# A sparse-attention and mixture-of-experts kernel: third gathers issued behind what frees their buffer, later zeros, and a first expert that reads no earlier results

## The chip, the cores and the metric

The kernel runs on one core of one Trainium2 chip. The metric is device time in microseconds (us) of one execution. TensorE (PE) multiplies matrices, VectorE (DVE) and ScalarE (ACT) do elementwise work, GpSimd (POOL) here issues all indirect DMAs (gathers and scatters by a list of row indices), and SyncE (SP) issues all other DMAs. Every engine works through its own instruction list in order: an instruction that waits holds up everything behind it on that engine.

## What is computed

Attention with two sparse masks over 8 batches of 576 tokens (8 heads of 64), then a mixture of 8 experts with the two best experts per token. Cut to what matters:

```python
scores = where(masks, scale * q @ k.T, -1e9)         # heads 0-3: a band of 32; heads 4-7: every 32nd key
x = softmax(scores) @ v                              # as 4608 tokens x 512
noisy = x @ w_gate + log1p(exp(x @ w_noise)) * noise # 4608 x 8
top2 = argpartition(-noisy, 2, axis=1)[:, :2]        # and their softmax: top2_w
out = zeros(4608, 512)
for e in range(8):
    for k in range(2):
        mask = top2[:, k] == e
        out[mask] += top2_w[mask, k, None] * (relu(x[mask] @ w1[e]) @ w2[e])
```

w1 is 512x1024 and w2 1024x512 for each expert.

## The kernel before

**Attention.** 32 units of work (batch, pair of heads, kind of mask). A unit loads q, k, v, transposes on PE, multiplies, takes exponentials on ACT, multiplies by v, and stores its part of x to DRAM (`x_dram`, L663). After the four units of a batch, `route` computes the gate and writes, by 12 indirect scatters on POOL (L824), the entries (token, weight) of that batch into each expert's list in DRAM (`tab`).

**Experts.** The list of an expert is cut into steps ("jobs"), listed in `SUBS` as (start, whole blocks of 128 tokens, tail, batches that must be known: `hb`). Seven jobs need only the first batches and are run while attention goes on. In order: job 0 (expert 0, 2 blocks, hb 2), job 1 (expert 0, 2 blocks, hb 4), job 2 (expert 1, 2 blocks, hb 4), job 3 (expert 1, 3 blocks, hb 5), jobs 4 to 6 (expert 2, 3, 2 and 2 blocks, hb 7). 25 more jobs need all 8 batches; 14 of these have a third block (two whole blocks and a third or a tail of 64). A job does the following:

- `gather` (L908): loads the list (L918), makes indices, and gathers the rows of x into tiles `xg`, one per block. The ring of `xg` has two places. Early jobs use one gather per block (L973), the others four (L959).
- `transposes` (L981): per block, transposes on PE into a PSUM bank (L998, early jobs) or on DVE (L1002, the others), and splits the result into a high part `xhi` (ACT, L1009) and a low part `xlo` (DVE, L1011). Rings `xhi`, `xlo` have one place, so they wait for the first layer of the job before.
- `layer1` (L1037), then `layer2` per block (L1099) on PE. Weights are loaded (L889, L892) and split in the same way (L894, L895).
- `previous` (L1077): gathers the rows of `out` that are to be added to. `weighted` (DVE, L1124): `out row + weight * product`. `scatter` (L1129): writes the rows back to `out`.
- The output is first filled with zeros, in 12 stores of 384 rows (L1183, 786432 bytes each, on SP). A gather or a scatter of the first `hb * 576` rows of `out` needs the zeros of these rows.

**The order of the work.** It is written down once, when the program is built. Each piece has an engine, a planned duration, a rank and what it depends on; `issue_all` simulates the engines with these durations and emits the pieces in the order in which they start in this plan. Among the pieces of an engine that could start within 120 ns of the first, the lowest rank goes first. Attention ranks are 10 per unit (40 per batch), expert ranks start at `ER` = 1000000. A piece also has a planned time before which it doesn't start (`t0`); a store of zeros has rank `ER - 1` and is `bulk`, which lets it start only where the planned load of the DMA engines has nearly run out. The semaphores are put in afterwards from what the emitted instructions read and write. So where the plan did not know of a dependency, the instruction waits in its place in the engine's list.

Three places matter here. When a tile is taken from a full ring, the plan makes the piece wait for the users that the tile to be replaced has *at that moment*:

```python
if len(r.hist) >= r.k:
    self.deps += r.hist[-r.k].users
```

In `gather`, all blocks of a job take their `xg` in one go, before `transposes` has made the pieces that read the first of them. For early jobs the list and its `gix` have the rank of the expert, while the list's load has the rank `20 * NP * (hb - 1) + 10 * NP` (NP = 2), which lies among attention's. And `previous` is made for every block, with `others` as the scatters of the other experts so far, which is an empty list for jobs 0 and 1.

Of the kernel before, what the change touches and what calls it, by code (L numbers as in the profile page):

```python
# [9 lines left out]
F32 = mybir.dt.float32  # L10
# [5 lines left out]
ALU = mybir.AluOpType  # L16
# [6 lines left out]
def kernel(  # L23
# [12 lines left out]
    nc = tc.nc  # L36
    B, H, S, D = q.shape
# [5 lines left out]
    NP = HL // 2  # L43
# [230 lines left out]
    def dve(n):  # L274
        return 75 + 1.04 * n

    def dma(fn, nbytes, rank, eng="SP", **kw):
        return Piece(eng, 690 if eng == "SP" else GAP, fn, rank, lat=nbytes, **kw)
# [137 lines left out]
    R = {}  # L416
# [461 lines left out]
            R[f"w{layer}{part}"] = ring(wring, [128, 512], F32R, f"w{layer}{part}", NF)  # L878
    R["wraw"] = ring(wring, [128, 512], F32, "wraw", 5)
    ER = 1000000  # L880
    ZC = 384

    def weights_of(e, layer, i, rank, turn=None):
# [18 lines left out]
    def experts(zero):  # L902
# [2 lines left out]
        known_tab = {n: [x for b in range(n) for x in scatters[b]] for n in range(1, B + 1)}  # L905
        G_, XH, HT = {}, {}, {}

        def gather(n, rank):  # L908
            e, (start, nb, tail, hb) = jobs[n]
            known = hb * S  # L910

            whole = hb < B
# [39 lines left out]
            if not whole:  # L952
                Piece("POOL", 360 if tail else 230, xindices, rank, read=[tx] + ([tx2] if tail else []), alloc=[gx],
                      expert=True)
            xs = []
            for i in () if whole else range(nb + (tail > 0)):
                xg = R["xg"].new()
                for g in range(4 if i < nb else tail // 32):
                    dma(lambda o, i=i, g=g, xg=xg: nc.gpsimd.indirect_dma_start(  # L959
                        out=xg.t[:, g, :], out_offset=None, in_=x_dram[:4 * known, :],  # L960
                        in_offset=bass.IndirectOffsetOnAxis(ap=gx.t[:, i, g:g + 1], axis=0)),
                        65536, rank, eng="POOL", read=[gx], after=known_stores[hb], expert=True,
                        **({"write": [xg]} if g else {"alloc": [xg]}))
                xs.append(xg)

            def indices(o):
                nc.gpsimd.tensor_scalar(gi.t[:, :nb], tb.t[:, :nb, 0], known - 1, None, op0=ALU.min)
                if tail:
                    nc.gpsimd.tensor_scalar(gi.t[:tail, nb:nb + 1], tb.t[:tail, nb, 0:1], known - 1, None, op0=ALU.min)
            Piece("POOL", 300 if tail else 170, indices, rank, read=[tb], alloc=[gi], expert=True)  # L970
            for i in range(nb) if whole else ():
                xg = R["xg"].new()
                dma(lambda o, i=i, xg=xg: nc.gpsimd.indirect_dma_start(  # L973
                    out=xg.t.rearrange("p g c -> p (g c)"), out_offset=None,
                    in_=x_dram.rearrange("(t q) c -> t (q c)", q=4)[:known, :],
                    in_offset=bass.IndirectOffsetOnAxis(ap=gi.t[:, i:i + 1], axis=0)),
                    262144, rank, eng="POOL", read=[gi], after=known_stores[hb], expert=True, alloc=[xg])
                xs.append(xg)
            G_[n] = (tb, gi, xs)

        def transposes(n, rank):  # L981


            e, (start, nb, tail, hb) = jobs[n]
            xh, xl = R["xhi"].new(), R["xlo"].new()
            XH[n] = (xh, xl)
            for i in range(nb + (tail > 0)):
                xg = G_[n][2][i]
                rows = 128 if i < nb else tail
                ng = rows // 32  # L990
                cols = slice(128 * i, 128 * i + rows)
                if hb < B:
                    xr = Slot()

                    def tr(o, xg=xg, xr=xr):
                        xv = xg.t.rearrange("p g c -> p (g c)").rearrange("p (x c) -> p c x", c=ND)
                        for c in range(ND):
                            nc.tensor.transpose(xr.t[:, 128 * c:128 * c + 128], xv[:, c, :], ident)  # L998
                    Piece("PE", 108 * ND, tr, rank, read=[xg], psum=xr, expert=True)
                else:  # L1000
                    xr = R["xr"].new()
                    Piece("DVE", 8 * rows, lambda o, xg=xg, xr=xr, ng=ng, rows=rows: nc.vector.transpose(  # L1002
                        xr.t.rearrange("p (c x) -> p c x", c=ND)[:, :, :rows].rearrange("p c (g i) -> p g c i", g=ng),
                        xg.t[:, :ng, :].rearrange("p g (i c) -> p g c i", c=ND)), rank, read=[xg], alloc=[xr], expert=True)
                how = "write" if i else "alloc"

                def view(xr=xr, rows=rows):
                    return xr.t.rearrange("p (c x) -> p c x", c=ND)[:, :, :rows]
                Piece("ACT", act(4 * rows), lambda o, view=view, cols=cols: nc.scalar.copy(  # L1009
                    xh.t[:, :, cols], view()), rank, read=[xr], expert=True, **{how: [xh]})  # L1010
                Piece("DVE", dve(4 * rows), lambda o, view=view, cols=cols: nc.vector.tensor_tensor(  # L1011
                    xl.t[:, :, cols], view(), xh.t[:, :, cols].bitcast(F32), ALU.subtract),
                      rank, read=[xr, xh], expert=True, **{how: [xl]})

        counts = {}

# [55 lines left out]
        def previous(n, i, rank, others):  # L1072
            e, (start, nb, tail, hb) = jobs[n]
            pv, gi = R["prev"].new(), G_[n][1]
            known = hb * S
            rows = 128 if i < nb else tail
            dma(lambda o: nc.gpsimd.indirect_dma_start(  # L1077
                out=pv.t[:rows, :], out_offset=None, in_=out[:known, :],
                in_offset=bass.IndirectOffsetOnAxis(ap=gi.t[:rows, i:i + 1], axis=0)),
                rows * 2048, rank, eng="POOL", read=[gi], alloc=[pv],  # L1080
                after=others + zero[:-(-known // ZC)], expert=True)
            return pv

        def layer2(n, i, rank, pv):
# [2 lines left out]
            rows = 128 if i < nb else tail  # L1087
            cols = slice(128 * i, 128 * i + rows)
            ps, tb = Slot(), G_[n][0]
            half = rows < 128  # L1090
            if half:

# [27 lines left out]
                Piece("PE", len(part) * 216, mm, rank, read=rd, expert=True, **({"write": [ps]} if c else {"psum": ps}))  # L1120

            def weighted(o):
                for r in range(0, 2 * rows if half else rows, rows):
                    nc.vector.scalar_tensor_tensor(pv.t[:rows, :], ps.t[r:r + rows, :], tb.t[:rows, i, 1:2].bitcast(F32),  # L1124
                                                   pv.t[:rows, :], op0=ALU.mult, op1=ALU.add)
            Piece("DVE", (1 + half) * dve(512), weighted, rank, read=[ps, tb, pv], write=[pv], expert=True)

            def scatter(o):
                st = nc.gpsimd.indirect_dma_start(  # L1129
# [4 lines left out]
                out_scatters[e].append(st)  # L1134
                return st
            out_done[e].append(dma(scatter, rows * 2048, rank, eng="POOL", read=[pv, tb], expert=True))

        def turn(n):
            hb = jobs[n][1][3]
            return None if hb == B else 20 * NP * (hb - 1) + 10 * NP  # L1140

        W2 = {}
        gather(0, ER)
# [36 lines left out]

    for c in range(NTOK // ZC):
        zero.append(dma(
            lambda o, c=c: nc.sync.dma_start(out[ZC * c:ZC * c + ZC, :].rearrange("(p c) (a d) -> p (c a) d", p=128, a=4),  # L1183
                                             zeros[:, None, :].to_broadcast([128, 4 * ZC // 128, 128])), 786432,
            ER - 1, t0=26000 + 10000 * c + 35000 * (c >= 5), bulk=True))
    LL = {0: loads(0, 0), 1: loads(1, 10)}
    KQ = {0: prep(0, LL[0], 0)}
    for u in range(NU):
# [93 lines left out]
```

## Time and profile before

| | us |
|---|---|
| runs shown: median (lowest to highest, 3 runs) | 1108.83 (1102.39 to 1113.18) |
| the profiled execution | 1104.51 |
| its span, first to last instruction | 1102.8 |
| PE busy in it | 1064.4 (97%) |
| DVE, ACT, POOL busy | 607.6, 432.8, 553.8 |

The three runs lie 1% apart. The profiled execution is near the lower end of them. A busy time is the time in which at least one instruction of that engine ran; PE's is modelled at the ends of its matmuls, and matmuls overlap. PEld is the loading of weights into PE. The granted clock (PEclk) is 1.00 at 2.4 GHz; a stretch that shows 0.57 was for a part of it at 1.2 GHz.

### The profile page before, as it was taken

The page shows a single profiled execution, that of the slowest core. Times are in us where ns is not written, and L with a number is a line of the kernel's source. Part 1 is how long each engine was busy: PE and PEld are TensorE (multiplying, and loading weights), DVE is VectorE, ACT ScalarE, POOL GpSimd, SP SyncE. Part 2 cuts the span into 40 slices and gives each one's busy share as a digit, 9 for nine tenths or more (in the row PEclk, how much of TensorE's full clock was granted, in tenths as well). Part 3 has the DMA queues.
Part 4 walks back from the last instruction along what each step waited for, and adds up shares of the span by engine and source line. Part 5 has one row for each costly group of instructions (what it writes and reads, how often), then busy time and mean ns, then how long its engine had stood idle before and what let it go on. Part 6 is the DMA issues. An engine that isn't in the chain of part 4 may idle for free.

```text
span 1102.8 us, 23359 instructions
## 1 busy us (share of the span) xinstructions
PE 1064.4 (97%) x8645; PEld 938.3 (85%) x8645; DVE 607.6 (55%) x1606; ACT 432.8 (39%) x1131; POOL 553.8 (50%) x734
## 2 busy tenths in 40 slices
PE   8898899999799999999999999999999999999995
PEld 7677678889688989898998989898988898898994
DVE  7789976776465223655673456345534553474341
ACT  6689975677353212423341224113312331142120
POOL 1045543510763455656676555655656464657530
PEclk8999999999899999999999999999999999999998
DMA  8999998887534332455554236223622452253210
GB/s 173 230 212 230 240 237 228 218 238 199 144 103 138 91 104 77 135 148 149 156 168 141 71 101 189 79 70 106 185 81 64 121 166 76 69 158 97 72 59 23
DMA packets 169482, 152.93 MB, mean 139 GB/s; under 512 B 52651, under 2 KB 137131, under 8 KB 169348
## 3 DMA queue, kind: packets, MB, share of 16 engines
q1 hardware_dynamic: 145028, 92.30, 33.4%
q0 software_dynamic: 24320, 58.87, 17.7%
q8 instruction: 82, 1.34, 0.5%
q14 instruction: 52, 0.43, 0.1%
HBM read 112.76 MB, written 39.39 MB: 138 GB/s over the span
## 4 chain that ended last, share of the span: by engine, by line
PE 82%; DVE 5%; issue 5%; DMA 4%; ACT 3%; POOL 0%; POOLq 0%; DVEq 0%; SPq 0%
PE bankE L1099 5%; PE bankF L1099 5%; PE bankG L1099 5%; PE bankC L1099 5%; PE bankG L1037 5%; PE bankF L1037 5%; PE bankA L1099 5%; PE bankH L1037 5%; PE bankC L1037 5%; PE bankA L1037 5%; PE bankD L1099 4%; PE bankB L1037 4%; PE bankD L1037 4%; PE bankE L1037 4%; PE bankH L1099 4%
## 5 line engine op out<-in xcount | busy, mean ns | idle before, releaser
L959 POOL DMA_INDIRECT xg<-x_dram,gxx x240 | 241.4, 1006 | 105.1 <-issue 55.7
L1129 POOL DMA_INDIRECT out_dram<-prev,tabt x80 | 82.1, 1026 | 103.7 <-DVE prev L1124 45.9
L1077 POOL DMA_INDIRECT prev<-out_dram,gix x80 | 77.3, 966 | 92.1 <-issue 39.5
L824 POOL DMA_INDIRECT tab<-ent,addr x96 | 92.2, 960 | 57.9 <-issue 15.6
L1002 DVE STREAM_TRANSPOSE xr<-xg 128x512 f32<-128x512 f32 (+1 forms) x64 | 66.3, 1037 | 12.7 <-DMA xg<-x_dram,gxx 11.2
L1009 ACT CAST xhi<-xr 128x512 fp32r<-128x512 f32 (+1 forms) x64 | 37.8, 591 | 69.9 <-DVE xr L1002 69.9
L894 ACT CAST w2hi<-wraw 128x512 fp32r<-128x512 f32 x80 | 47.4, 619 | 29.2 <-PE bankA L1108 7.4
L895 DVE TENSOR_TENSOR w1lo<-wraw,w1hi 128x512 fp32r<-128x512 f32 x80 | 54.7, 686 | 3.5 <-ACT w1hi L894 1.0
L895 DVE TENSOR_TENSOR w2lo<-wraw,w2hi 128x512 fp32r<-128x512 f32 x80 | 52.7, 684 | 3.5 <-ACT w2hi L894 2.2
L1011 DVE TENSOR_TENSOR xlo<-xr,xhi 128x512 fp32r<-128x512 f32 (+1 forms) x64 | 42.1, 658 | 18.4 <-ACT xhi L1009 17.2
L894 ACT CAST w1hi<-wraw 128x512 fp32r<-128x512 f32 x80 | 49.0, 614 | 1.4 <-DMA wraw<-in_moe_w_dram 1.2
L973 POOL DMA_INDIRECT xg<-x_dram,gix x16 | 16.8, 1050 | 58.4 <-PE bankD L998 42.8
L1056 ACT ACTIVATE hhi<-bankG 128x256 fp32r<-128x256 f32 (+2 forms) x34 | 14.3, 421 | 70.9 <-PE bankG L1037 70.9
L1037 PE MATMUL bankG<-xhi,w1hi 128*128 128x256 f32 (+3 forms) x136 | 41.2, 303 | 0.0
L1037 PE MATMUL bankG<-xhi,w1lo 128*128 128x256 f32 (+3 forms) x136 | 40.3, 296 | 0.0
L1037 PE MATMUL bankG<-xlo,w1hi 128*128 128x256 f32 (+3 forms) x136 | 40.1, 295 | 0.0
L1037 PE MATMUL bankF<-xhi,w1hi 128*128 128x256 f32 (+3 forms) x132 | 39.9, 302 | 0.0
L1037 PE MATMUL bankH<-xhi,w1hi 128*128 128x256 f32 (+3 forms) x132 | 39.7, 301 | 0.0
L1037 PE MATMUL bankA<-xhi,w1hi 128*128 128x256 f32 (+3 forms) x132 | 39.6, 300 | 0.0
L1037 PE MATMUL bankC<-xhi,w1hi 128*128 128x256 f32 (+3 forms) x132 | 39.6, 300 | 0.0
L1037 PE MATMUL bankF<-xhi,w1lo 128*128 128x256 f32 (+3 forms) x132 | 39.4, 298 | 0.0
L1037 PE MATMUL bankF<-xlo,w1hi 128*128 128x256 f32 (+3 forms) x132 | 39.3, 298 | 0.0
(666 smaller groups left out, 3573.1 us busy)
## 6 DMA issues: line engine op xcount, KB each, us to landing
wraw<-in_moe_w_dram SPq DMA_DIRECT2D x160, 256.0 KB
out_dram<-zeros SPq DMA_DIRECT2D x12, 768.0 KB
ks<-in_k_dram SPq DMA_DIRECT2D x15, 320.0 KB
qs<-in_q_dram SPq DMA_DIRECT2D x15, 320.0 KB
vraw<-in_v_dram SPq DMA_DIRECT2D x30, 160.0 KB
raw<-in_k_dram SPq DMA_DIRECT2D x16, 288.0 KB
v_l<-in_v_dram SPq DMA_DIRECT2D x16, 288.0 KB
raw<-in_q_dram SPq DMA_DIRECT2D x16, 288.0 KB
```

What stands on the lines that cost most here:

```text
L824: st = nc.gpsimd.indirect_dma_start(out=tab, out_offset=bass.IndirectOffsetOnAxis(ap=s["addr"].t[:, t, kk:kk + 1], axis=0), in_=s["ent"].t ...
L894: Piece("ACT", act(512) + 30, lambda o: nc.scalar.copy(hi.t, raw.t), rank, read=[raw], alloc=[hi], expert=True)
L895: Piece("DVE", dve(512), lambda o: nc.vector.tensor_tensor(lo.t, raw.t, hi.t.bitcast(F32), ALU.subtract), rank, read=[raw, hi], alloc=[lo] ...
L959: dma(lambda o, i=i, g=g, xg=xg: nc.gpsimd.indirect_dma_start(out=xg.t[:, g, :], out_offset=None, in_=x_dram[:4 * known, :], in_offset=bas ...
L973: dma(lambda o, i=i, xg=xg: nc.gpsimd.indirect_dma_start(out=xg.t.rearrange("p g c -> p (g c)"), out_offset=None, in_=x_dram.rearrange("(t ...
L1002: Piece("DVE", 8 * rows, lambda o, xg=xg, xr=xr, ng=ng, rows=rows: nc.vector.transpose(xr.t.rearrange("p (c x) -> p c x", c=ND)[:, :, :row ...
L1009: Piece("ACT", act(4 * rows), lambda o, view=view, cols=cols: nc.scalar.copy(xh.t[:, :, cols], view()), rank, read=[xr], expert=True, **{h ...
L1011: Piece("DVE", dve(4 * rows), lambda o, view=view, cols=cols: nc.vector.tensor_tensor(xl.t[:, :, cols], view(), xh.t[:, :, cols].bitcast(F ...
L1037: nc.tensor.matmul(ps.t[:, :width], a.t[:, 128 * d:128 * d + 128], c.t[:, d, :width], start=(m == 0), stop=(m == len(todo) - 1))
L1077: dma(lambda o: nc.gpsimd.indirect_dma_start(out=pv.t[:rows, :], out_offset=None, in_=out[:known, :], in_offset=bass.IndirectOffsetOnAxis( ...
L1099: nc.tensor.matmul(ps.t, HT[n, f][p[0]].t[:, cols], W2[n][f][p[1]].t, start=(m == 0), stop=(m == len(todo) - 1))
L1129: st = nc.gpsimd.indirect_dma_start(out=out[:known, :], out_offset=bass.IndirectOffsetOnAxis(ap=tb.t[:rows, i, 0:1], axis=0), in_=pv.t[:ro ...
```

## The change

Four edits.

1. `gather` now makes only the first two blocks of a job. The third is made by a function `rows_of`, which `transposes` calls after it has made the pieces of the block whose place the third takes. Nothing else about the gather changes.
2. In early jobs, the index computation and the gathers get the rank that the load of their list has (`turn(n)`), instead of the expert's.
3. The 12 stores of zeros get new earliest times in the plan. Before: 26, 36, 46, 56, 66, 111, 121, 131, 141, 151, 161, 171. After: 95, 105, 115, 140, 150, 160, 185, 195, 215, 228, 240, 280 (in thousands of ns).
4. Jobs 0 and 1 no longer gather rows of `out`: `previous` returns an empty tile, and `weighted` writes weight times product into it. In the plan this piece now waits for the zeros.

```diff
+    ZERO_AT = (95, 105, 115, 140, 150, 160, 185, 195, 215, 228, 240, 280)
...
         def gather(n, rank):
             e, (start, nb, tail, hb) = jobs[n]
+            rank = rank if hb == B else turn(n)
...
-            xs = []
-            for i in () if whole else range(nb + (tail > 0)):
+            def rows_of(i):
                 xg = R["xg"].new()
+                if whole:
+                    dma(lambda o: nc.gpsimd.indirect_dma_start(
...
+                        262144, rank, eng="POOL", read=[gi], after=known_stores[hb], expert=True, alloc=[xg])
+                    return xg
                 for g in range(4 if i < nb else tail // 32):
...
-                xs.append(xg)
+                return xg
+            xs = [] if whole else [rows_of(i) for i in range(2)]
...
-            for i in range(nb) if whole else ():
-                xg = R["xg"].new()
...
-            G_[n] = (tb, gi, xs)
+            if whole:
+                xs = [rows_of(i) for i in range(2)]
+            G_[n] = (tb, gi, xs, rows_of)
...
                       rank, read=[xr, xh], expert=True, **{how: [xl]})
+                if i + 2 < nb + (tail > 0):
+
+                    xs.append(rows_of(i + 2))
...
             pv, gi = R["prev"].new(), G_[n][1]
+            if not others:
+                return pv
...
+            first = jobs[n][0] == jobs[0][0] and hb < B
...
             def weighted(o):
-                for r in range(0, 2 * rows if half else rows, rows):
+                if first:
+                    nc.vector.tensor_scalar(pv.t, ps.t, tb.t[:, i, 1:2].bitcast(F32), None, op0=ALU.mult)
+                for r in () if first else range(0, 2 * rows if half else rows, rows):
...
-            Piece("DVE", (1 + half) * dve(512), weighted, rank, read=[ps, tb, pv], write=[pv], expert=True)
+            Piece("DVE", (1 + half) * dve(512), weighted, rank, expert=True,
+                  **({"read": [ps, tb], "alloc": [pv], "after": zero[:-(-known // ZC)]} if first else
+                     {"read": [ps, tb, pv], "write": [pv]}))
...
-            ER - 1, t0=26000 + 10000 * c + 35000 * (c >= 5), bulk=True))
+            ER - 1, t0=ZERO_AT[c] * 1000, bulk=True))
```

## Rows read from the trace of the kernel before

**Rows 1.** The page's first line: span and count of instructions.
```profile
span 1102.8 us, 23359 instructions
```

**Rows 2.** Windows by stage: length, busy per engine, clock, DMA share, GB/s.
```profile
core 0: us, PE busy (x) PEld busy (x) DVE busy (x) ACT busy (x) POOL busy (x), PEclk, DMA share, GB/s
60.00:165.00 105.00, 93.04 (x1541) 74.87 (x1539) 90.81 (x356) 91.53 (x292) 52.84 (x101) 0.97 1.05 234
165.00:260.00 95.00, 94.99 (x1208) 83.24 (x1206) 69.09 (x252) 64.55 (x185) 29.63 (x50) 1.00 0.88 229
260.00:345.00 85.00, 78.78 (x804) 68.11 (x796) 45.38 (x154) 39.30 (x115) 40.08 (x68) 0.94 0.53 141
345.00:1090.00 745.00, 745.00 (x4339) 670.40 (x4339) 357.72 (x659) 198.02 (x416) 423.31 (x480) 1.00 0.37 111
```

**Rows 3.** Timeline of POOL from 234 to 298 us: start, length, instruction, wait.
```profile
234.79 0.20 POOL L812 COPY ent<-wt 96x12 f32<-96x12 f32 x1 [0.80 <-DVE wt L806]
276.63 0.97 POOL L973 DMA_INDIRECT xg<-x_dram,gix  x1 [41.65 <-PE bankD L998]
277.91 0.93 POOL L824 DMA_INDIRECT tab<-ent,addr  x1 [0.21 <-POOL spacer L823]
...
291.33 0.91 POOL L824 DMA_INDIRECT tab<-ent,addr  x1 [0.21 <-issue]
...
297.41 1.00 POOL L1077 DMA_INDIRECT prev<-out_dram,gix  x1 [2.54 <-DMA out_dram<-prev,tabt]
```

**Rows 4.** Timelines of PE and DVE from 262 to 311 us: the long waits.
```profile
281.48 0.72 PE L998 MATMUL bankC<-ident,xg 128*128 128x128 f32 x4 [2.29 <-DMA xg<-x_dram,gix]
301.65 0.39 PE L550 MATMUL bankF<-mask_s,twin 64*64 64x288 bf16 x1 [3.68 <-DVE prev L1124]
300.85 0.75 DVE L1124 SCALAR_TENSOR_TENSOR prev<-bankF,tabt,prev 128x512 f32<-128x512 f32 x1 [6.76 <-DMA prev<-out_dram,gix]
```

**Rows 5.** Windows of 5 us, columns as in rows 2.
```profile
150.00:155.00 5.00, 5.00 (x84) 4.69 (x84) 3.19 (x12) 1.87 (x7) 3.00 (x6) 0.66 1.08 204
...
285.00:290.00 5.00, 5.00 (x67) 4.27 (x67) 3.27 (x11) 2.23 (x4) 4.01 (x9) 0.80 0.47 118
...
300.00:305.00 5.00, 3.35 (x45) 2.83 (x45) 3.92 (x12) 0.23 (x2) 4.22 (x9) 0.57 0.57 166
305.00:310.00 5.00, 5.00 (x37) 3.75 (x36) 1.54 (x8) 2.06 (x10) 4.13 (x10) 0.75 0.07 15
```

**Rows 6.** Timeline of SP's queue: five of the lines of the zeros.
```profile
46.42 0.62 SPq L1183 DMA_DIRECT2D out_dram<-zeros  x1
66.36 1.23 SPq L1183 DMA_DIRECT2D out_dram<-zeros  x1
177.27 2.81 SPq L1183 DMA_DIRECT2D out_dram<-zeros  x2
201.93 0.58 SPq L1183 DMA_DIRECT2D out_dram<-zeros  x1
272.02 1.52 SPq L1183 DMA_DIRECT2D out_dram<-zeros  x2
```

**Rows 7.** Chain that ended last, 60 to 165 us: start, length, link.
```profile
71.36 4.89 DMA vraw<-in_v_dram
```

**Rows 8.** Timelines of SP, POOL and PE: how job 0 begins.
```profile
118.67 0.68 SPq L918 DMA_DIRECT2D tabt<-tab  x1
138.01 1.41 POOL L973 DMA_INDIRECT xg<-x_dram,gix  x1 [0.40 <-POOL gix L967]
158.76 0.36 PE L1037 MATMUL bankA<-xhi,w1hi 128*128 128x256 f32 x1
```

**Rows 9.** The page's costliest groups, and waits of POOL (total, times, longest).
```profile
L1077 POOL DMA_INDIRECT prev<-out_dram,gix x80 | 77.3, 966 | 92.1 <-issue 39.5
POOL xg L959 <- DVE xr L1002: 19.3, 15, 3.2
```

**Rows 10.** A late job: DVE's last split, and the chain's first-layer matmuls.
```profile
883.18 0.69 DVE L1011 TENSOR_TENSOR xlo<-xr,xhi 128x512 fp32r<-128x512 f32 x1
887.86 2.08 PE bankE L1037 x12
```

More of the change, by code (lines that the diff above doesn't have):

```diff
@@ L906, in experts, with turn @@
         G_, XH, HT = {}, {}, {}
+        def turn(n):
+            hb = jobs[n][1][3]
+            return None if hb == B else 20 * NP * (hb - 1) + 10 * NP
         def gather(n, rank):
             e, (start, nb, tail, hb) = jobs[n]
+            rank = rank if hb == B else turn(n)
             known = hb * S
@@ L954, in gather @@
                       expert=True)
-            xs = []
-            for i in () if whole else range(nb + (tail > 0)):
+            def rows_of(i):
                 xg = R["xg"].new()
+                if whole:
+                    dma(lambda o: nc.gpsimd.indirect_dma_start(
+                        out=xg.t.rearrange("p g c -> p (g c)"), out_offset=None,
+                        in_=x_dram.rearrange("(t q) c -> t (q c)", q=4)[:known, :],
+                        in_offset=bass.IndirectOffsetOnAxis(ap=gi.t[:, i:i + 1], axis=0)),
+                        262144, rank, eng="POOL", read=[gi], after=known_stores[hb], expert=True, alloc=[xg])
+                    return xg
                 for g in range(4 if i < nb else tail // 32):
-                    dma(lambda o, i=i, g=g, xg=xg: nc.gpsimd.indirect_dma_start(
+                    dma(lambda o, g=g: nc.gpsimd.indirect_dma_start(
                         out=xg.t[:, g, :], out_offset=None, in_=x_dram[:4 * known, :],
@@ L970, in gather @@
             Piece("POOL", 300 if tail else 170, indices, rank, read=[tb], alloc=[gi], expert=True)
-            for i in range(nb) if whole else ():
-                xg = R["xg"].new()
[L973 to L978, printed above, removed]
-            G_[n] = (tb, gi, xs)
+            if whole:
+                xs = [rows_of(i) for i in range(2)]
+            G_[n] = (tb, gi, xs, rows_of)
         def transposes(n, rank):
@@ L987, in transposes @@
             for i in range(nb + (tail > 0)):
-                xg = G_[n][2][i]
+                xs, rows_of = G_[n][2:]
+                xg = xs[i]
                 rows = 128 if i < nb else tail
@@ L1136, in layer2 @@
             out_done[e].append(dma(scatter, rows * 2048, rank, eng="POOL", read=[pv, tb], expert=True))
-        def turn(n):
-            hb = jobs[n][1][3]
-            return None if hb == B else 20 * NP * (hb - 1) + 10 * NP
         W2 = {}
```

## The prediction, made before the changed kernel was run

> **What bounds the kernel now.** I read the windows by stage first, then the waits inside the stage that has a gap, then POOL's timeline, because all three parts of the change move work on POOL or in front of it. From 345 us to the last matmul at 1090 PE is busy 745.00 of 745.00 us at clock 1.00 [rows 2]. Nothing that the change does can be worth anything there as long as PE stays fed; the work behind 345 us is a block that starts sooner or later. So the question is only how much PE time is lost ahead of 345 us. Between 165 and 260 it is nothing, 94.99 of 95.00. It is 105.00 - 93.04 = 12.0 us between 60 and 165, and 85.00 - 78.78 = 6.2 us between 260 and 345 [rows 2]. To this comes the clock: behind the gaps the granted clock is lower, 0.80, 0.57 and 0.75 of the upper level (2.4 GHz) in the 5 us windows from 285, 300 and 305 [rows 5], a mean of stretches at it and at 1.2 GHz, and PE does that much less in its busy time: 0.20 x 5.00 + 0.43 x 3.35 + 0.25 x 5.00 = 3.7 us. Likewise 0.34 x 5.00 = 1.7 us from 150 to 155 [rows 5].
>
> The gap after 260 has one cause that can be followed. At 234.79 POOL has the entries of the sixth batch ready, but next in its list stands the third gather of job 3, which waits 41.65 us, until PE has transposed the block that frees its place, and issues at 276.63. Behind it stood the batch's 12 table scatters (277.91 to 291.33), job 1's output scatters, and at 297.41 the first gather of earlier results for job 2 [rows 3]. DVE then waits 6.76 us for that gather to land, and PE 3.68 us for DVE, since the banks that attention needs are freed behind it. The third gather itself lands late for PE too: 2.29 us at 281.48 [rows 4].
>
> **The change part by part.**
>
> Third gathers. For job 3 the gather moves behind the transposes in the plan, so POOL does the 12 scatters, job 1's scatters and job 2's gathers of results in the 41.65 us. Those gathers then land long before 294 us, when DVE asked: the waits of 6.76 and 3.68 us go, and the clock behind them, 1.4 + 1.2 us. The 2.29 us should go too: the plan now knows when the third block arrives, and PE has second-layer products of job 2 to put there. If it doesn't, 2.3 us and perhaps the 1.0 us of clock behind it stay. Bounds: 0, if the same wait comes back elsewhere, and 6.2 + 3.7 = 9.9, the whole loss of this stage. I take 9, near the upper end, because two named waits (6.0 us) and the clock drops that follow them are nearly all of it. What is late next is the third gather itself, 4.85 us from issue (276.63) to PE's first use (281.48) [rows 3, 4]; second-layer work covers it. Job 4 has the same form and costs less. In the 14 late jobs POOL now doesn't stand before a third gather: its waits for DVE's transposes of 19.3 us in total [rows 9] go. PE is full there, so 0.
>
> The earlier rank of early jobs. Job 0's list is loaded at 118.67 but its first gather issues at 138.01, after the third batch's scatters, and its first product runs at 158.76 [rows 8]. With a rank among attention's the gather goes ahead of those scatters: perhaps 15 of the 19.3 us sooner, and what POOL now does later is 12 scatters by two gathers, about 2.5 us, for which nobody waits until job 1. PE gets filler for 15 us of a stage in which it idles 12.0/105 of the time: 1.7 us, and the drop at 150 (1.7 us) may not come. Bounds 0 and 3.4; I take 2.
>
> The zeros. Stores issued at 46.42 and 66.36 move behind 95 in the plan; most of the others already left later than their new times, as far as 272.02 [rows 6]. That takes 2 x 0.786 MB off the DMA engines before 95 us; at the 234 GB/s of rows 2 it is 6.7 us. Right behind the second of them a load of v of 160 KB lies 4.89 us on the chain [rows 7], though at that rate it is 0.7 us of transfer. But DVE (90.81) and ACT (91.53 of 105 us) are nearly as full as the DMA engines, so not all of it shows. Bounds 0 and 6.7; I take 3. A rule of the Trainium skill speaks against even that (DMA: Bandwidth & Descriptors, "Issuing engines are not separate DMA queues"): DMAs of all issuing engines run interleaved on the same 16 engines, so the zeros now meet the expert gathers. No row here times a zero beside a gather; the share of 1.05 [rows 2] says only that there is no free room. By the rule alone this term would be 0 and the sum 11 instead of 14.
>
> The gathers that are left out. Four POOL instructions of 966 ns [rows 9], 3.9 us, and 4 x 0.26 MB = 1.05 MB of reads, all between 165 and 260, where PE has no gap and POOL is 31% busy: 0. They also pay for the zeros: +1.57 - 1.05 MB is 2.3 us at 229 GB/s on a stage of 95 us with a share of 0.88 [rows 2], still not full. If that cover were gone, the cost would be those 2.3 us. The multiply replaces a multiply-add on DVE, four times under 1 us, DVE being 69.09 of 95 busy: 0. The new wait on zeros: if the two early stores take the next places in SP's list, the third zero is the one that left fifth, at 177.27 [rows 6], 18.5 us behind job 0's first product at 158.76 [rows 8]. A scatter needs the whole first layer and a block of the second, in between attention's work. Only if job 0 starts 15 us sooner could POOL stand there, for a few us, ahead of table scatters that nobody waits for yet: 0.
>
> Sum: 9 + 2 + 3 = 14 us. The profiled execution took 1104.5 (span 1102.8 [rows 1] and 1.7 around it), which gives 1090.5. It lies 4.3 us under the median of the three runs, 1108.8, from which the same sum gives 1094.8. I predict 1093, between the two.
>
> **The rivals.** *More than that* (0.17). The attention stage is paced by the DMA engines alone, share 1.05 [rows 2], and gives back the 6.7 us and more of its 12.0 us of idle PE. With 9.9 behind it: about 22 us, 1085 from the middle of the two bases (1107). Against it: DVE and ACT at 87%. A rule of the skill makes it larger (Perfetto Trace Analysis, "Identifying the Most-Contended Engine"): PE's busy time is a poor measure of how near it is to its limit, the share of weight loads a better one. That share is 0.71 between 60 and 165 against 0.90 behind 345 [rows 2], by which the stage loses 105 - 74.87/0.90 = 22 us instead of 12, and the time could come to 1075.
>
> *The wait comes back in another place* (0.25). The plan puts the gather behind transposes that it thinks early, and POOL or DVE waits again; or the zeros become the wait. Job 3 needs eight of them. The one at 201.93 was the eighth to leave; if two places are lost, the eighth is one that left at 272.02 [rows 6], landing after 275, and job 3's gathers of results could be asked for up to 40 us sooner than now. A block of 15 us on POOL, at the 9.9 us per 41.65 of this trace, gives back 4 us. With no gain ahead of 165 either: 0 to 6 us gained, 1101 to 1108.
>
> *Slower* (0.13). In the 14 late jobs the third gather is placed later than its place is free. In the job at 887.86 the last split ends at 883.87, 4.0 us before PE needs it [rows 10]. A block is four gathers of about 1 us [rows 9] and their spacing; if a scatter that waits for PE gets ahead of them and they come more than 4 us later, PE stands, and each us beyond that point costs 14 us in all. At 6 us it is 28, less the 14 gained: 1107 + 14 = 1121. Against it: the gathers have a lower rank than the scatters of the job before, and POOL is 57% busy there.
>
> **How the numbers follow.** The forecast, 8 to 20 us gained, has 0.45. The range takes it, a part of "more" and most of "the wait comes back": 1080 to 1109, leaving out 0.2. The measurement can tell about 1%, 11 us of 1108.8, from no change: faster is below 1097.7, which most of the forecast (0.36 of 0.45) and all of "more" meet: 0.53. Same: 0.34. Slower: 0.13.
>
> **What the profile will show.** Right: no POOL wait of over 10 us for a transpose between 230 and 300; the sixth batch's scatters right behind their entries; DVE's wait for the results' gather gone; PE's idle between 260 and 345 under 2 us, clock 1.00; the first expert product before 150 us; the window of 745 us of full PE starting 10 to 15 us sooner and equally long. Wrong: a gap in PE behind 345, a scatter of job 0 or 1 waiting for zeros, a gap before 165 as large as now. I would be wrong in size if the stage before 165 has other limits than the DMA load.

## The result and the profile after

The changed kernel takes 1097.04 us (median of 20 runs, 1092.48 to 1103.98), the kernel before 1107.72 (20 runs, 1102.39 to 1113.18): a ratio of 0.9906, 95% interval 0.9892 to 0.9920, or 10.7 us less. The forecast was 14 us less and 1093.

First the span and the busy times of the profiled execution after (line 1 and section 1 of its page). It took 1092.48 us, the shortest of the 20 runs:

```profile
span 1090.8 us, 23344 instructions
PE 1058.4 (97%) x8645; PEld 933.9 (86%) x8645; DVE 606.2 (56%) x1614; ACT 434.4 (40%) x1123; POOL 544.1 (50%) x730
```

The span is 12.0 us shorter than before [rows 1]. PE's busy time fell from 1064.4 to 1058.4, though its matmuls are the same, so 6.0 of the 12.0 us are idle time and 6.0 are busy time. How much of the busy time is clock is not shown: an estimate, busy time times the missing part of the clock, summed over windows of 5 us, gives 12.0 us before and 9.0 after. Where the idle time went, the windows by stage tell (length, busy time per engine with instructions, granted clock, DMA share, GB/s):

```profile
60.00:165.00 105.00, 91.80 (x1562) 73.61 (x1562) 91.89 (x370) 90.48 (x280) 46.38 (x93) 0.95 0.97 221
165.00:260.00 95.00, 95.00 (x1178) 83.08 (x1177) 68.16 (x252) 65.35 (x191) 41.20 (x76) 1.00 0.91 230
260.00:345.00 85.00, 85.00 (x840) 73.78 (x839) 51.40 (x190) 42.39 (x115) 33.77 (x59) 1.00 0.58 157
345.00:1078.00 733.00, 733.00 (x4281) 660.73 (x4281) 349.07 (x614) 193.75 (x407) 413.25 (x464) 1.00 0.38 112
```

Against [rows 2]: between 260 and 345 us PE's idle went from 6.2 us to nothing and the clock from 0.94 to 1.00. Behind that the block of full PE is as dense as before and ends at 1078 instead of 1090. But between 60 and 165 us nothing was won: idle 13.2 us (12.0 before) and clock 0.95 (0.97), although the DMA share fell from 1.05 to 0.97. Two of the three terms of the forecast lay in that stage, and a gap there "as large as now" was a sign of being wrong that the prediction had named.

POOL's timeline after, where [rows 3] showed the wait of 41.65 us (start, length, instruction, idle before and what ended it):

```profile
228.91 0.20 POOL L812 COPY ent<-wt 96x12 f32<-96x12 f32 x1 [2.47 <-DVE wt L806]
232.39 1.01 POOL L824 DMA_INDIRECT tab<-ent,addr  x1 [3.26 <-issue]
...
254.10 1.24 POOL L824 DMA_INDIRECT tab<-ent,addr  x1 [1.15 <-DMA vraw<-in_v_dram]
255.64 1.02 POOL L1150 DMA_INDIRECT out_dram<-prev,tabt  x1 [0.31 <-issue]
258.04 1.00 POOL L1150 DMA_INDIRECT out_dram<-prev,tabt  x1 [1.38 <-DVE prev L1141]
264.59 0.99 POOL L1092 DMA_INDIRECT prev<-out_dram,gix  x1 [5.54 <-DVE mx L584]
...
280.86 0.97 POOL L966 DMA_INDIRECT xg<-x_dram,gix  x1 [2.20 <-PE bankH L787]
```

The sixth batch's scatters go right behind its entries (232.39 to 254.10 instead of 277.91 to 291.33), then job 1's output, then job 2's gathers of results at 264.59 instead of 297.41. The third gather of job 3 stands behind all of that, at 280.86, and waits 2.20 us.

Job 0 after, from the timelines of POOL, DVE and PE (first gather; split of the first and of the second block; first product):

```profile
127.66 1.08 POOL L966 DMA_INDIRECT xg<-x_dram,gix  x1 [1.11 <-issue]
143.49 0.68 DVE L1021 TENSOR_TENSOR xlo<-bankE,xhi 128x512 fp32r<-128x512 f32 x1
163.41 0.66 DVE L1021 TENSOR_TENSOR xlo<-bankF,xhi 128x512 fp32r<-128x512 f32 x1
164.20 0.36 PE L1050 MATMUL bankE<-xhi,w1hi 128*128 128x256 f32 x1
```

The gather issues 10 us sooner than in [rows 8], but the first product comes 5 us later: the second block's low part runs on DVE only at 163.41, and the product 0.8 us behind it. The sign "the first expert product before 150 us" did not come.

### The profile page after: what moved, and what is told of

The parts are those of the page before. It is cut to its first block, busy times and chain, and to the rows that moved or that the text cites. A ratio compares the mean times of both kernels' runs of the same rounds, so it can differ in the third digit from the quotient of the medians.

```text
span 1090.8 us, 23344 instructions
## 1 busy us (share of the span) xinstructions
PE 1058.4 (97%) x8645; PEld 933.9 (86%) x8645; DVE 606.2 (56%) x1614; ACT 434.4 (40%) x1123; POOL 544.1 (50%) x730
## 4 chain that ended last, share of the span: by engine, by line
PE 89%; DVE 4%; ACT 3%; DMA 2%; issue 1%; POOL 0%; POOLq 0%; DVEq 0%; ACTq 0%; SPq 0%
PE bankA L1116 6%; PE bankH L1116 6%; PE bankA L1050 5%; PE bankD L1116 5%; PE bankG L1116 5%; PE bankB L1050 5%; PE bankH L1050 5%; PE bankE L1050 5%; PE bankD L1050 5%; PE bankG L1050 5%; PE bankB L1116 5%; PE bankE L1116 4%; PE bankF L1050 4%; PE bankC L1050 4%; PE bankC L1116 4%; PE bankF L1116 3%
## 5 line engine op out<-in xcount | busy, mean ns | idle before, releaser
L1092 POOL DMA_INDIRECT prev<-out_dram,gix x76 | 73.3, 964 | 85.8 <-issue 30.2
L1012 DVE STREAM_TRANSPOSE xr<-xg 128x512 f32<-128x512 f32 (+1 forms) x64 | 66.4, 1038 | 18.1 <-DMA xg<-x_dram,gxx 16.1
L1021 DVE TENSOR_TENSOR xlo<-xr,xhi 128x512 fp32r<-128x512 f32 (+1 forms) x64 | 42.1, 658 | 18.4 <-ACT xhi L1019 17.2
L1050 PE MATMUL bankA<-xhi,w1hi 128*128 128x256 f32 (+3 forms) x140 | 42.3, 302 | 0.0
L1050 PE MATMUL bankA<-xhi,w1lo 128*128 128x256 f32 (+3 forms) x140 | 41.6, 297 | 0.0
L1069 ACT ACTIVATE hhi<-bankB 128x256 fp32r<-128x256 f32 (+2 forms) x33 | 14.1, 426 | 69.0 <-PE bankB L1050 68.9
L1050 PE MATMUL bankA<-xlo,w1hi 128*128 128x256 f32 (+3 forms) x140 | 41.5, 296 | 0.0
L1050 PE MATMUL bankB<-xhi,w1hi 128*128 128x256 f32 (+3 forms) x132 | 40.2, 304 | 0.0
L1050 PE MATMUL bankE<-xhi,w1hi 128*128 128x256 f32 (+3 forms) x132 | 39.6, 300 | 0.0
L1050 PE MATMUL bankB<-xhi,w1lo 128*128 128x256 f32 (+3 forms) x132 | 39.4, 298 | 0.0
L1050 PE MATMUL bankH<-xhi,w1lo 128*128 128x256 f32 (+3 forms) x132 | 39.4, 298 | 0.0
L1050 PE MATMUL bankB<-xlo,w1hi 128*128 128x256 f32 (+3 forms) x132 | 39.3, 297 | 0.0
```

Source lines behind the costliest of these rows:

```text
L1050: nc.tensor.matmul(ps.t[:, :width], a.t[:, 128 * d:128 * d + 128], c.t[:, d, :width], start=(m == 0), stop=(m == len(todo) - 1))
L1069: Piece("ACT", act(width) + 30, lambda o: nc.scalar.activation(hh.t[:, :width], ps.t[:, :width], AF.Relu), rank, read=[ps], alloc=[hh], ex ...
L1092: dma(lambda o: nc.gpsimd.indirect_dma_start(out=pv.t[:rows, :], out_offset=None, in_=out[:known, :], in_offset=bass.IndirectOffsetOnAxis( ...
```

## The experiments

The twelve kernels ran in three groups of four, on three chips. The kernel before took 1105.92, 1109.35 and 1151.65 us there, so kernels of different groups are compared by their ratios only, and those of the third group among themselves. Ratios of different groups are a weak comparison too: the cost of edit 3 differs from chip to chip by more than most of what is compared.

**Edit 1 alone (third gathers).** The other three edits left out.

```diff
+            def rows_of(i):
...
+            if whole:
+                xs = [rows_of(i) for i in range(2)]
...
+                if i + 2 < nb + (tail > 0):
+                    xs.append(rows_of(i + 2))
```

> The kernel before with the first edit alone: the third gather of a job is made behind the transposes that free its place; ranks, zeros and gathers of results as before. Theory (the gain is the removed wait of 41.65 us on POOL and what came of it, 6.2 us of idle PE and 3.7 us of clock between 260 and 345 us): 9 to 11 us less than before, about 1097; PE busy 85 of 85 us between 260 and 345, clock 1.00, no wait of POOL over 10 us for a transpose. Rival (the gain comes from less work on POOL and the DMA engines ahead of 165 us): 0 to 3 us less, though the wait is gone.

Measured 1095.30 us, ratio 0.9908 (0.9890 to 0.9927): 10.6 us less, the whole gain of the change. Its windows of the first and third of these stages:

```profile
60.00:165.00 105.00, 94.18 (x1571) 76.77 (x1567) 94.03 (x367) 92.93 (x297) 54.72 (x102) 0.95 1.04 234
260.00:345.00 85.00, 85.00 (x890) 74.06 (x889) 54.50 (x204) 43.56 (x126) 33.19 (x55) 1.00 0.54 153
```

The gap behind 260 is closed as in the changed kernel. The DMA share before 165 stays at 1.04, and PE idles there 10.8 us, less than with a share of 0.97.

**Edits 2 to 4 (edit 1 undone).** From the changed kernel, all blocks of a job are gathered in one go again.

```diff
-            xs = [] if whole else [rows_of(i) for i in range(2)]
...
+            for i in range(nb) if whole else ():
+                xg = R["xg"].new()
```

> The changed kernel without the first edit: all three blocks of a job are again gathered in one go; ranks, zeros and gathers left out as in the changed kernel. Theory: within 3 us of before (1107), since the third gather of job 3 stands in POOL's list again: a wait of 30 us or more for a transpose, and a gap of 4 us or more in PE behind it. Rival (less work on POOL and DMA): 8 to 11 us less than before, about 1098.

Measured 1106.37 us, ratio 1.0015 (0.9999 to 1.0032): nothing. From its waits between 160 and 345 us (engine, line, what was waited for: us in total, times, longest):

```profile
POOL xg L981 <- PE bankH L1006: 39.9, 1, 39.9
DVE prev L1138 <- DMA prev<-out_dram,gix: 9.9, 1, 9.9
PE bankD L505 <- DVE prev L1138: 6.5, 1, 6.5
```

It is the sequence of [rows 3, 4] once more, POOL, then DVE, then PE. Ranks, zeros and fewer gathers don't touch it.

**Edit 3 alone (zeros).**

```diff
-            ER - 1, t0=26000 + 10000 * c + 35000 * (c >= 5), bulk=True))
+            ER - 1, t0=ZERO_AT[c] * 1000, bulk=True))
```

> The kernel before with the new times of the 12 zero stores alone. If the stage from 60 to 165 us is paced by the DMA engines, the two early stores (1.57 MB at 234 GB/s) are worth up to 6.7 us: idle PE there falls from 12.0 to 6 or less, time about 1101 to 1103. If DVE and ACT pace it (87% busy), idle stays at 11 to 13 us and the time within 3 us of before.

Measured 1121.97 us, ratio 1.0139 (1.0116 to 1.0161): slower by 16.1 us in the medians, which no theory had expected. Its waits between 160 and 345 us:

```profile
POOL xg L974 <- DVE hlo L1062: 41.1, 1, 41.1
DVE prev L1125 <- DMA prev<-out_dram,gix: 20.3, 1, 20.3
PE bankD L785 <- DVE ohs L776: 13.1, 1, 13.1
```

The first line names DVE, but what frees the place is the transposes on PE, which run from 302.90 to 303.55; the gather follows at 303.82. POOL's wait for the third place is no longer than before, but it holds up more: DVE stands 20.3 us behind it instead of 6.76, and PE 13.1 instead of 3.68 [rows 4]. Between 60 and 165 us:

```profile
60.00:165.00 105.00, 92.68 (x1524) 75.02 (x1522) 90.68 (x364) 93.52 (x293) 49.68 (x95) 0.93 0.97 217
```

PE idles 12.3 us: with two zero stores less in that stage (those that left at 66.36 and 160.60 before) as much as before.

The kernel with edits 2 to 4 ran on the same chip and took 1106.37 us, 15.6 us less than edit 3 alone. So edits 2 and 4, each worth nothing alone (next two paragraphs), took back nearly the whole loss of edit 3 there. Which of them did it is not separated.

**Edit 4 alone (jobs 0 and 1 gather no results).**

```diff
+            if not others:
+                return pv
...
+                if first:
+                    nc.vector.tensor_scalar(pv.t, ps.t, tb.t[:, i, 1:2].bitcast(F32), None, op0=ALU.mult)
```

> The kernel before with the fourth edit alone: jobs 0 and 1 gather no rows of the output. Theory: four gathers of 0.97 us and 1.05 MB less in a stage in which PE has no gap: within 2 us of before, the wait of POOL for the third gather still there. Rival (POOL's load matters in itself): 4 us or more less.

Measured 1106.38 us, ratio 1.0009 (0.9994 to 1.0024): nothing, as expected. POOL still waited 42.1 us for the third place.

**Edit 2 alone (rank).**

```diff
+            rank = rank if hb == B else turn(n)
```

> The kernel before with edit 2 alone (early jobs' index computation and gathers with the rank of their list's load). The prediction's term: first product before 150 us, PE idle from 60 to 165 us down from 12.0 to about 10, 2 us gained, about 1104. Theory now: the splits behind the gather still have the expert's rank and wait on DVE behind attention's work, so the first product does not come before 155 us, PE's idle in that stage stays within 1.5 us of 12.0, and the time stays within 3 us of the kernel before. POOL's wait of about 40 us for the third gather's place stays.

Measured 1108.45 us, ratio 0.9998 (0.9977 to 1.0019): nothing, but my reason for it was wrong. The first product did come early, at 145.09 us. Between 60 and 165 us PE idles 8.5 us (12.0 before), more than the prediction's term asked. Four lines of this kernel, PE's first product, two windows of 15 us and job 0's first scatter on POOL, and behind them the same two windows before:

```profile
145.09 0.39 PE L1042 MATMUL bankB<-xhi,w1hi 128*128 128x256 f32 x1
135.00:150.00 15.00, 14.65 (x232) 12.38 (x231) 12.45 (x37) 12.92 (x41) 9.29 (x15) 1.00 1.04 266
165.00:180.00 15.00, 11.68 (x163) 9.05 (x165) 10.27 (x32) 10.46 (x33) 7.88 (x14) 0.89 0.97 214
191.93 1.02 POOL L1134 DMA_INDIRECT out_dram<-prev,tabt  x1 [10.72 <-DMA out_dram<-zeros]
```

```profile
135.00:150.00 15.00, 11.86 (x185) 9.48 (x185) 13.52 (x69) 12.33 (x39) 7.36 (x14) 1.00 1.09 254
165.00:180.00 15.00, 15.00 (x200) 13.72 (x197) 8.52 (x30) 8.30 (x25) 4.74 (x8) 1.00 0.86 220
```

Before, PE was busy 11.86 us from 135 to 150 and 15.00 from 165 to 180. Now it is 14.65 and 11.68: the expert work fills the first gap, job 0's first layer is used up by 165, and the gap stands 30 us further on. The second layer begins only at 180.74:

```profile
180.74 0.50 PE L1104 MATMUL bankG<-w2hi,hhi 128*128 128x512 f32 x1
```

Its products do not read the gathered results (issued at 178.26 and 180.26); only DVE's addition does, and that waits for PE at 190.90. The last part of the layer's input is ready on DVE at 169.88 (169.47 and 0.41 us), so PE's place for these products in its list is later than their inputs; why the plan put them there is open. The wait of 10.72 us in front of the scatter is put down to a store of zeros, issued at 189.41, but the rows that it writes are made by DVE until 191.65. The zeros can have held it by 0.28 us at most, so this kernel does not show the prediction's rival of the zeros as the wait.

**Edits 1 and 3.** Whether the 16.1 us of edit 3 are the old wait or the zeros themselves.

> The kernel before with edits 1 and 3 (third gathers, zeros), without edit 4. The later zeros alone cost 15 us. Theory: that loss was the third gather's block on POOL again, at another place in the list (DVE waited 20.3 us and PE 13.1 us behind it), and not a wait for zeros; with edit 1 it is gone: 1094 to 1099, no POOL wait over 10 us for a place of xg, no DVE wait over 5 us for earlier results. Rival: the gathers of earlier results wait for the late zeros, which only edit 4 takes away: then DVE's wait of about 20 us stays and the time is 15 us above edit 1 alone, about 1110.

Measured 1103.06 us, ratio 0.9952 (0.9925 to 0.9979). The time lies between both theories. The long waits are gone (POOL's longest for a place of `xg` is below 5 us, DVE's of 20 us too), so about two thirds of the loss were the wait that edit 1 takes away, if the two chips may be compared. But against edit 1 in the early jobs in the same group (next, 1097.70) the late zeros cost 5.4 us. The two intervals just meet, and the kernels also differ in the late jobs, where edit 1 is worth nothing that can be seen (next). Job 0 shows where: second split and first product of this kernel, then of the next one:

```profile
166.32 0.68 DVE L1014 TENSOR_TENSOR xlo<-bankC,xhi 128x512 fp32r<-128x512 f32 x1
168.07 0.58 PE L1043 MATMUL bankB<-xhi,w1hi 128*128 128x256 f32 x1
```

```profile
158.88 0.69 DVE L1013 TENSOR_TENSOR xlo<-bankG,xhi 128x512 fp32r<-128x512 f32 x1
159.48 0.36 PE L1042 MATMUL bankA<-xhi,w1hi 128*128 128x256 f32 x1
```

With late zeros the first product is 8.6 us later. In the two profiles the span is 6.2 us longer with them, of which 5.1 are PE busy time: the clock is 0.90 instead of 0.92 between 60 and 165 us, and 0.96 instead of 1.00 between 165 and 260. Job 0's second gather of results went at 210.60, 22 us behind the first, and its scatters at 217.24 and 223.14 (211.93 and 213.25 with the old zero times).

**Edit 1 in the early jobs alone.** The late jobs gather in one go.

```diff
-            xs = [] if whole else [rows_of(i) for i in range(2)]
+            xs = [] if whole else [rows_of(i) for i in range(nb + (tail > 0))]
...
-                if i + 2 < nb + (tail > 0):
+                if len(xs) <= i + 2 < nb + (tail > 0):
```

> The kernel before with edit 1 in the early jobs only (jobs 3 and 4); the late jobs make all their gathers in one go as before. Theory: PE is full behind 345 us, so the 14 late jobs give nothing and this is as fast as edit 1 in all jobs, 1093 to 1098. Rival: part of the gain is POOL's 19.3 us of waits in the late jobs; then this gives only a part of the 10.6 us, 1099 to 1104.

Measured 1097.70 us, ratio 0.9900 (0.9873 to 0.9927): as much as edit 1 in all jobs (0.9908). The 14 late jobs give nothing that can be seen; jobs 3 and 4 carry it.

**The changed kernel, with the rank for the splits too.** In the early jobs the transposes and both splits get the rank that edit 2 gives to the gathers.

```diff
         def transposes(n, rank):
...
             e, (start, nb, tail, hb) = jobs[n]
+            rank = rank if hb == B else turn(n)
```

> The changed kernel, and in the early jobs the transposes and splits too get the rank of the list's load. In the changed kernel the second block's xlo ran on DVE at 163.44 us, 17 us behind its xhi, and the first product at 164.20 right behind it. Theory: with the rank the first product comes before 157 us and PE has filler sooner, but DVE and ACT are about 87% busy in that stage and attention's own pieces come later for it: no gain beyond 2 us, 1095 to 1099. Rival (the prediction's second term with its cover mended): 1.7 to 3.4 us less than the changed kernel, 1093.5 to 1095.5, with PE's idle from 60 to 165 us 2 us or more lower.

Measured 1093.55 us, ratio 0.9846 (0.9818 to 0.9875). This interval lies below that of the changed kernel (0.9892 to 0.9920): about 0.6%, or 6 us, more than either theory had. But the two ran in different groups. In its own group it lies 4.2 us below edit 1 in the early jobs (the intervals just meet) and 9.5 us below edits 1 and 3. Its second split, its first product and its stage from 60 to 165 us:

```profile
146.24 0.69 DVE L1022 TENSOR_TENSOR xlo<-bankE,xhi 128x512 fp32r<-128x512 f32 x1
146.95 0.39 PE L1051 MATMUL bankG<-xhi,w1hi 128*128 128x256 f32 x1
60.00:165.00 105.00, 90.55 (x1420) 74.22 (x1422) 85.06 (x343) 86.02 (x263) 45.00 (x89) 0.97 0.93 208
```

The product comes 17 us sooner than in the changed kernel, as both theories said. What the trace doesn't show is where the 6 us are: the profiled execution (1096.43, the longest of four) has PE idle 14.4 us between 60 and 165, no less than the changed kernel. The gain rests on four times and on ratios of different groups; that it is one over the changed kernel is likely, not shown, and its place stays open.

**Four combinations on the third chip.** Edits 1 and 4; edits 1, 3 and 4 (the changed kernel without edit 2); edits 1 and 2; and the kernel of the last paragraph with the old zero times:

```diff
-            ER - 1, t0=ZERO_AT[c] * 1000, bulk=True))
+            ER - 1, t0=26000 + 10000 * c + 35000 * (c >= 5), bulk=True))
```

> The kernel before with edits 1 and 4 (third gathers; jobs 0 and 1 gather no results), old zero times, old ranks. Theory: edit 4 alone gave nothing (1106.4), and with edit 1 it gives nothing either, because jobs 0 and 1 start as late as before: 1094 to 1099. Rival: the gathers left out give a gain of their own once the third gather no longer stands in POOL's list: 1090 to 1093.

> The changed kernel without edit 2 (edits 1, 3 and 4). Edits 1 and 3 together gave 5 us less than edit 1 alone: there job 0's second gather of results went at 210.60 us, 22 us behind its first, and its scatters at 217 and 223. Theory: edit 4 takes these gathers away and with them the 5 us: 1094 to 1100. Rival: the late zeros cost their 5 us in another way: 1101 to 1105.

> The kernel before with edits 1 and 2. Edit 2 alone brought the first product to 145 us, and PE's idle from 60 to 165 us from 12.0 to 8.5, but a gap of 3.3 us came between 165 and 180, where job 0's second layer waited for its gathers of results (178.26, 180.26 us). Theory: the same happens here, the filler is used up sooner and the gap moves: 1094 to 1099, as edit 1 alone. Rival (the prediction's term): 2 us or more below edit 1 alone, 1091 to 1094.

> The changed kernel with the early jobs' transposes and splits at the rank of the list's load (1093.55 us, ratio 0.985), and the zeros at their old times (edit 3 undone). If late zeros only cost, as with edit 1 alone: the same or faster, 1089 to 1094, ratio 0.980 to 0.985. Rival (the prediction's third term, 3 us for the zeros out of the stage from 60 to 95 us): 1095 to 1098, ratio 0.987 to 0.990.

Measured, beside 1151.65 us of the kernel before:

| | us | ratio (95% interval) |
|---|---|---|
| edits 1, 4 | 1130.02 | 0.9831 (0.9791 to 0.9872) |
| edits 1, 3, 4 | 1144.07 | 0.9923 (0.9899 to 0.9947) |
| edits 1, 2 | 1133.36 | 0.9825 (0.9781 to 0.9869) |
| edits 1, 2, 4, splits ranked | 1128.79 | 0.9804 (0.9768 to 0.9840) |

The times that had been expected were worked out for the other chips and don't apply. One pair is a clean comparison: the first two differ in edit 3 alone, and the late zeros cost 14.1 us. The theory that edit 4 makes late zeros harmless falls, at least on this chip; that the whole change lost nothing by them (0.9906 beside 0.9908 for edit 1 alone) must then come from edit 2 or from the chip. The 15.6 us that edits 2 and 4 took back without edit 1 fit edit 2, but no kernel here separates the two. The stage from 60 to 165 us of the two, first with the old zero times, then with the new ones:

```profile
60.00:165.00 105.00, 87.17 (x1290) 67.63 (x1288) 78.25 (x313) 77.89 (x240) 43.63 (x82) 0.87 0.86 198
```

```profile
60.00:165.00 105.00, 89.29 (x1231) 72.47 (x1231) 72.57 (x274) 78.29 (x238) 38.43 (x75) 0.77 0.79 182
```

With fewer bytes on the DMA engines DVE has done less, 274 instructions instead of 313, and the clock is lower. The first product moved from 179.98 to 189.98 us. The other three kernels of the table can't be told apart. Edit 1 alone did not run on this chip, so whether edit 2 or 4 adds to it is open; so is what the ranked splits give with the old zero times on the first two chips.

## Why the prediction was right or wrong

**What bounds the kernel: right.** All of the gain lies ahead of 345 us, and from 165 us on PE is full in the profile after, 733.00 of 733.00 us behind 345.

**Third gathers: right, in mechanism and about in size.** 9 us were forecast. Edit 1 alone gave 10.6 us, with an interval of 8.1 to 12.2. Each sign came: scatters behind their entries, DVE's wait gone, no idle PE and clock 1.00 from 260 to 345. The 2.29 us for the third gather's landing are gone too. One detail was wrong and cost nothing: POOL's waits in the late jobs for DVE's transposes did not go. The waits of the changed kernel behind 345 us list them:

```profile
POOL xg L973 <- DVE xr L1012: 20.6, 17, 3.2
```

That is 20.6 us instead of 19.3 [rows 9]. POOL still reaches a third gather before DVE has done the transpose that frees its place. PE is full there, so neither number is worth anything, which the kernel with edit 1 in the early jobs alone shows.

**Rank: 2 us forecast, nothing measured alone; in the change its share is not separated.** The term had two steps, and each failed in one of the kernels. The first is "the gather goes ahead of those scatters: perhaps 15 of the 19.3 us sooner", and from there directly to "PE gets filler for 15 us". In the changed kernel the gather came 10 us sooner and the product 5 us later. Between gather and product stand two transposes and four splits, and `transposes` keeps the expert's rank. I had read the ranks of the gather and of its list, but not those of the pieces behind it. How many DVE instructions the trace has up to the start of the second split, and when it and the first product run:

| | DVE instructions before it | second split, us | first product, us |
|---|---|---|---|
| before | 534 | 158.30 | 158.76 |
| edit 2 alone | 458 | 143.72 | 145.09 |
| edit 3 alone | 548 | 166.32 | 167.78 |
| changed kernel | 555 | 163.41 | 164.20 |
| changed, splits ranked | 455 | 146.24 | 146.95 |

In each row the product follows the split by 0.5 to 1.5 us. With edit 2 alone the plan happens to find room for the split early; together with the other edits it stands 21 instructions later than before. The second step is that filler which comes sooner is time gained. With edit 2 alone the first step came true, product and idle time both, and it gave nothing: job 0's first layer was used up by 165 us, the second began at 180.74, and 3.3 us of the idle time came between them. I had counted the filler that comes sooner, not the one that is missing later.

**Zeros: 3 us forecast, a loss measured.** In three comparisons on one chip each it cost 16.1, 5.4 and 14.1 us; edit 3 is the only difference in the first and the third, and the second differs in the late jobs too. Beside edits 2 and 4 the first of these losses is gone. The step that failed is the reading of [rows 2]: a DMA share of 1.05 was taken as a load that holds attention up, so that 6.7 us of transfer less must show in part. Of the two stores that were meant, only that of 66.36 us lies in the stage from 60 to 165 whose rate and idle time were used; that of 46.42 lies ahead of it. The runs take load off (0.97), and PE idles as long as before or longer. The v loads behind which I had seen it [rows 7] are no quicker either. In the changed kernel, a link of the chain and the first line of the zeros:

```profile
59.54 7.12 DMA vraw<-in_v_dram
171.63 1.79 SPq L1200 DMA_DIRECT2D out_dram<-zeros  x2
```

A v load of 7.12 us starts at 59.54, with no zeros issued before 171.63. "I would be wrong in size if the stage before 165 has other limits than the DMA load" was the right reservation; DVE (91.89 of 105 us) and ACT (90.48) are as full as before. What the transfers alone cost is not shown, since moving the zeros also moved the order of the other work. The rule of the Trainium skill that was weighed there (DMA: Bandwidth & Descriptors, "Issuing engines are not separate DMA queues") would, as weighed, have set this term to 0, nearer than my 3. It says only that the DMA engines are shared, and no run here shows a zero store that slows a gather.

How the later zeros cost is shown in part. With them (edits 1 and 3 against edit 1 in the early jobs) the third batch's routing stands 11 instructions later in DVE's order, and job 0's second split 14. The batch's entries on POOL, with late zeros and with the old times:

```profile
122.28 0.20 POOL L812 COPY ent<-wt 96x12 f32<-96x12 f32 x1 [12.22 <-DVE wt L806]
```

```profile
115.81 0.20 POOL L812 COPY ent<-wt 96x12 f32<-96x12 f32 x1 [5.29 <-DVE wt L806]
```

The other profiles agree. From the first batch's entries to the third's it takes 66.7 to 71.2 us in the five kernels with late zeros (third chip left out), and 59.7 to 63.4 in the five with the old times. So attention falls behind there although the DMA engines have less to do, and expert work starts later. By the sixth batch, 170.0 to 180.0 us against 178.2 to 185.9, attention has made it up, but at the price of expert work. A job of two blocks has 64 first-layer matmuls that read `w1hi`. By the sixth batch's entries all eight kernels with the old zero times have run 128 of them. With late zeros it is 64 with edit 3 alone and with edits 1 and 3, 92 with edits 1, 3 and 4, 118 with edits 2 to 4 and in the changed kernel, and 128 with the splits ranked too. The three kernels in which a loss by late zeros was measured are those with 64 and 92. What is missing there runs later, where PE is full. The order is the plan's: with other zero times it expects other loads to land first. That the plan expects too much of the freed DMA engines is argued, not shown.

**The sum.** 9 + 2 + 3 was forecast; by the runs the change is 10.6 from edit 1 and about nothing from the other three together (1.0015 without edit 1, and the changed kernel at 0.9906 beside edit 1 at 0.9908). On the one chip where it can be read, that nothing is a loss by edit 3 and as large a gain by edits 2 and 4 beside it, and neither was forecast. The forecast was 4 us too good: two terms of 5 us did not come, the first was 1.6 too small, and the base was 0.7 too low (1107.72 less 14 is 1093.7). So it is near because its largest term was right; the other two were not.

**The rivals.** "More than that" rested on a stage paced by DMA, and fell with it. So did the larger form of it, by the Trainium skill's Perfetto Trace Analysis ("Identifying the Most-Contended Engine"): the share of weight loads between 60 and 165 is 73.61 of 105, 0.70 (0.71 before), and the run shows nothing of the 22 us. "The wait comes back" did not happen in the changed kernel (POOL's longest wait for a place there is 8.7 us). The zeros as the wait show in no run: the one long wait that the profiles put down to them, in edit 2 alone, is theirs for 0.28 us at most. "Slower" did not come: PE is full behind 345.

## What to carry to other kernels

An in-order engine that takes all its buffers in one go waits for the last of them in front of everybody else's work; placing the claim behind what frees the buffer was worth 10.6 us here, and only in the two jobs where PE had a gap behind it. A high busy share of the DMA engines is no proof that transfers set the pace: here it fell from 1.05 to 0.97 and the stage did not shorten. Where a plan made from expected transfer times sets the order, a moved transfer moves the other work too, so compare the order before the times. Where a piece is to start sooner, follow the rank of every piece up to the one that is to profit, and ask what will fill the gap from which it was taken. And a wait that the profile puts down to one instruction may have had another end: check when the data themselves were written.

## What the runs showed of the hardware

- Closing the gap brought the clock back too: from 260 to 345 us the granted clock rose from 0.94 to 1.00 in the changed kernel and with edit 1 alone. Over the whole span PE's busy time for the same matmuls also varies without that: with the gap still there it was 1064.4 us before, 1061.8 with edit 4 alone and 1057.9 with edits 2 to 4 (1058.4 in the changed kernel). So the 6.0 us between before and after are not the gap's alone.
- Chips differ more than the change is worth: the kernel before took 1105.92, 1109.35 and 1151.65 us on three. On the third, the two instructions that were compared are as long as elsewhere (the weight split on DVE 676 ns against 680 on the second, the high part on ACT 617 against 616), but the seventh batch's entries come at 307.45 us instead of 288.15 in a kernel that differs only in the zeros' times. What is slower there stays open.
